# SwiGLU on one core: tile 2 of w1 held back by a dummy sigmoid, tile 3 moved behind the first w1 piece, w3's halves on both queues

## The chip, the core and the metric

One core of a Trainium2 chip runs the whole program. The metric is the device time of one execution in microseconds (us). Times inside a profile count from the first instruction of the program; that span is some 1.8 us shorter than the device time. All inputs start in HBM, and the output ends there.

Most executions of a kernel lie close together, but some are more than 1.5% above the fastest of the same kernel; these are called slow.

## The reference

```python
# x: 32x32x512, w1 and w3: 512x1792, w2: 1792x512, all bf16
gate = jnp.einsum("bsd,df->bsf", x, w1)
up   = jnp.einsum("bsd,df->bsf", x, w3)
h    = silu(gate) * up
out  = jnp.einsum("bsf,fd->bsd", h, w2)
```

The contraction over 512 is cut into four tiles of 128. "Tile 2" below means the third of these (rows 256 to 383 of w1).

## The kernel before

SP and ScalarE each own a DMA queue. The kernel loads the first 256 rows of x on both queues, then the first 512 columns of w1 and of w3 in pieces, and starts on those with half a block of x. The rest of the weights follows while TensorE is already busy.

```python
    one = nc.const_aps.tensor(1.0, [P, 1], bf16)
    table = consts.tile([P, 1], fp32, name="table")

    load_x(nc.sync, 0, 1)
    load_x(nc.scalar, 1, 2)
    load_w(nc.sync, w1_sb, w1_v, 0, FK, 0, 2)      # "w1a": tiles 0, 1, 256 KB
    nc.scalar.activation(table[:], one, SIGMOID)   # dummy: brings the sigmoid table in early
    load_w(nc.scalar, w1_sb, w1_v, 0, FK, 2, DT)   # "w1b": tiles 2, 3, 256 KB
    load_w(nc.sync, w3_sb, w3_v, 0, FK, 0, 2)      # "w3a"
    load_w(nc.sync, w3_sb, w3_v, 0, FK, 2, DT)     # "w3b"
    nc.sync.dma_start_transpose(out=xT[:, :, HB:NB], in_=x_flat[HB:NB, :])
    # ... rest of w1 and w3, the other x rows, w2, all on SP

    keep_warm(6, NB)                               # six matmuls on constants
    # ... x's first 256 rows turned on TensorE, copied to xT by VectorE and ScalarE
    for dt in range(DT):                           # 16 gate matmuls of 256 columns
        for fo in range(FK):
            project(gates[fo], w1_sb, fo, 0, HB, [dt])
    for dt in range(DT):                           # 16 up matmuls
        for fo in range(FK):
            project(ups[fo], w3_sb, fo, 0, HB, [dt])
    # ... second half of the block (needs the DMA-transposed x), then all other blocks, then w2
```

## Time and profile before

| | before |
|---|---|
| device time, median of 6 | 82.59 us (82.09 to 82.73) |
| span of the profiled execution | 80.6 us |
| TensorE busy | 75.9 us, 94% |
| w1a issued, landed | 1.20, 5.02 |
| first gate matmul | 5.07 |
| first up matmul | 6.83 |
| first 256 rows of x ready in xT | 4.1 to 4.76 |

"Issued" is the start of the issuing instruction; "landed" is that start plus the time to landing that the DMA view gives for it. TensorE never waits noticeably after 5.07, so the span is the start of the weight matmuls plus a fixed 75.5 us. The prediction below shows the lines of the chain; in it the up matmuls start at 6.99, because a piece of the chain begins where the one before it ends. TensorE's own timeline (start, length, what, in brackets the idle time before) has the start itself:

```profile
5.07 1.92 PE L123 MATMUL gate_ps<-xT,w_sb 128*128 128x256 bf16 x16 [0.94 <-DMA w_sb<-in_w_dram]
6.83 1.91 PE L123 MATMUL up_ps<-xT,w_sb 128*128 128x256 bf16 x16
```

### The profile page before, as it was taken

To read this page: it belongs to the slowest core of one execution; us is meant where nothing else is said; L and a number is where in the kernel's file an instruction comes from. 1 tells how busy PE (TensorE), PEld (TensorE's weight loads), DVE (VectorE), ACT (ScalarE), POOL (GpSimd) and SP (SyncE) were. 2 spreads that over 40 slices of the span, in tenths; PEclk is the share of its full clock that TensorE was granted. 3 is DMA by queue.
4 is the path that set the end of the run, shared out by engine and by line. 5 is a ranking of instruction groups with operands and counts; after the bars stand their busy time and mean duration, and the time that the engine had idled before them with its cause. 6 is when DMAs were issued, how large, how long until landed. Compare 5 with 4: busy or idle time off the path is not lost.

```text
span 80.6 us, 1063 instructions
## 1 busy us (share of the span) xinstructions
PE 75.9 (94%) x404; PEld 38.8 (48%) x410; DVE 39.4 (49%) x61; ACT 23.2 (29%) x39; POOL 0.7 (1%) x6
## 2 busy tenths in 40 slices
PE   6959999999999999999999999999999999999960
PEld 2348984444444444444444444444444444444850
DVE  0110189999888878878868878872000000000040
ACT  4430274223432223432223432220220220220200
POOL 3000000000000000000000000000000000000000
PEclk9999999999999999999999999999999999999999
DMA  1999999989910000000000000000101102001120
GB/s 24 271 365 273 350 370 370 295 185 355 355 47 0 0 0 0 0 0 0 8 4 0 0 0 0 0 4 0 38 27 65 41 24 73 34 31 65 36 78 17
DMA packets 9893, 7.67 MB, mean 95 GB/s; under 512 B 3744, under 2 KB 9888, under 8 KB 9888
## 3 DMA queue, kind: packets, MB, share of 16 engines
q1 hardware_dynamic: 9472, 7.21, 29.6%
q10 hardware_dynamic: 416, 0.39, 1.4%
q8 instruction: 3, 0.05, 0.3%
q14 instruction: 2, 0.02, 0.1%
HBM read 5.77 MB, written 1.05 MB: 85 GB/s over the span
## 4 chain that ended last, share of the span: by engine, by line
PE 90%; DMA 5%; issue 1%; SPq 0%; DVE 0%; DVEq 0%
PE gate_ps L123 30%; PE o_ps L171 30%; PE up_ps L123 30%; DMA w_sb<-in_w_dram 5%; SPq L62 0%; DVE o_sb L180 0%; DVEq L180 0%
## 5 line engine op out<-in xcount | busy, mean ns | idle before, releaser
L123 PEld LDWEIGHTS <-w_sb 128*128 128x128 bf16 x256 | 25.0, 98 | 24.2 <-DMA w_sb<-in_w_dram 1.1
L123 PE MATMUL gate_ps<-xT,w_sb 128*128 128x512 bf16 (+1 forms) x126 | 28.7, 352 | 1.0 <-DMA w_sb<-in_w_dram 0.9
L123 PE MATMUL up_ps<-xT,w_sb 128*128 128x512 bf16 (+1 forms) x126 | 28.7, 352 | 0.1
L133 ACT ACTIVATE sig<-gate_ps 128x512 f32<-128x512 f32 x28 | 16.7, 597 | 32.0 <-PE gate_ps L123 29.7
L171 PE MATMUL o_ps<-w_sb,hT 128*128 128x512 bf16 (+2 forms) x138 | 24.3, 336 | 0.1
L135 DVE TENSOR_TENSOR t<-gate_ps,sig 128x512 f32<-128x512 f32 x28 | 19.3, 689 | 9.5 <-ACT sig L133 9.5
L136 DVE TENSOR_TENSOR hT<-t,up_ps 128x512 bf16<-128x512 f32 x28 | 19.3, 688 | 3.3 <-PE gate_ps L123 0.5
L171 PEld LDWEIGHTS <-hT 128*128 128x128 bf16 x140 | 12.6, 98 | 12.0
L180 DVE CAST o_sb<-o_ps 128x128 bf16<-128x128 f32 (+1 forms) x3 | 1.0, 336 | 22.3 <-PE o_ps L171 22.3
L182 ACT CAST o_sb<-o_ps 128x512 bf16<-128x512 f32 x7 | 4.1, 586 | 17.9 <-PE o_ps L171 17.9
L94 PE MATMUL warm_ps<-const-bfloat16-1.0 128*128 128x512 bf16 x6 | 2.7, 626 | 0.8 <-PEq L202 0.8
L116 DVE CAST xT<-pT 128x128 bf16<-128x128 f32 (+1 forms) x2 | 0.7, 358 | 3.7 <-PE pT L106 3.7
L94 PEld LDWEIGHTS <-const-bfloat16-1.0 128*128 128x128 bf16 x6 | 0.7, 136 | 1.8 <-issue 1.8
L74 ACT ACT_TABLE_LOAD x1 | 1.3, 1283 | 1.2 <-PEq L202 1.2
L116 ACT CAST xT<-pT 128x128 bf16<-128x128 f32 (+1 forms) x2 | 0.9, 426 | 1.2 <-PE pT L106 1.2
L106 PEld LDWEIGHTS <-x_sb 128*128 128x128 bf16 x8 | 0.5, 101 | 0.9 <-DMA x_sb<-in_x_dram 0.8
L106 PE MATMUL pT<-ident,x_sb 128*128 128x128 bf16 x8 | 0.7, 230 | 0.0
masks.py:199 POOL TENSOR_SCALAR_AFFINE_SELECT ident<-ident 128x128 bf16<-128x128 bf16 x1 | 0.3, 294 | 0.1
masks.py:197 POOL MEMSET ident<- 128x128 bf16 x1 | 0.2, 205 | 0.3 <-POOLq L202 0.3
L74 ACT ACTIVATE table<-const-bfloat16-1.0 128x1 f32<-128x1 bf16 x1 | 0.2, 203 | 0.0
L202 POOL MEMSET const-bfloat16-1.0<- 128x1 bf16 x1 | 0.1, 103 | 0.0
L202 POOL MEMSET const-uint8-127<- 128x1 uint8 x1 | 0.1, 103 | 0.0
(2 smaller groups left out, 0.2 us busy)
## 6 DMA issues: line engine op xcount, KB each, us to landing
w_sb<-in_w_dram SPq DMA_DIRECT2D x2, 896.0 KB, 7.0
w_sb<-in_w_dram SPq DMA_DIRECT2D x2, 768.0 KB, 8.1
w_sb<-in_w_dram SPq DMA_DIRECT2D x2, 512.0 KB, 5.8
out_dram<-o_sb SPq DMA_DIRECT2D x7, 128.0 KB, 1.7
w_sb<-in_w_dram SPq DMA_DIRECT2D x3, 256.0 KB, 4.3
w_sb<-in_w_dram ACTq DMA_DIRECT2D x1, 256.0 KB, 4.0
x_sb<-in_x_dram ACTq DMA_DIRECT2D x1, 128.0 KB, 2.8
x_sb<-in_x_dram SPq DMA_DIRECT2D x1, 128.0 KB, 2.6
```

Of the source, the lines that this page charges most:

```text
L74: nc.scalar.activation(table[:], one, SIGMOID)
L94: nc.tensor.matmul(warm_ps[:, 0:cols], lhsT=one.to_broadcast([P, P]), rhs=one.to_broadcast([P, cols]), start=True, stop=True,)
L106: nc.tensor.matmul(pT[:, i, j, :], lhsT=x_sb[:, nt, dt * P : (dt + 1) * P], rhs=ident[:], start=True, stop=True,)
L116: copy(xT[:, dts[0] : dts[-1] + 1, nts[0] * P : (nts[-1] + 1) * P], pT[:].rearrange("p d t c -> p d (t c)"),)
L123: nc.tensor.matmul(ps[:, c0 : c0 + n1 - n0], lhsT=w_sb[:, dt, fo * P : (fo + 1) * P], rhs=xT[:, dt, n0:n1], start=(dt == 0), stop=(dt == D ...
L133: nc.scalar.activation(sig[:], gate_ps[:], SIGMOID)
L135: nc.vector.tensor_mul(t[:], gate_ps[:], sig[:])
L136: nc.vector.tensor_mul(hT[:, fo, nb * NB : (nb + 1) * NB], t[:], up_ps[:])
L171: nc.tensor.matmul(o_ps[:], lhsT=hT[:, fo, nt * P : (nt + 1) * P], rhs=w2_sb[:, fo, c0 : c0 + DB], start=(fo == 0), stop=(fo == FT - 1),)
L180: nc.vector.tensor_copy(o_sb[:], o_ps[:])
L182: nc.scalar.copy(o_sb[:], o_ps[:])
L202: nc = _bacc.Bacc("TRN2", target_bir_lowering=False, num_devices=1)
```

## The change

The intent: w1a is what TensorE waits for, and it shares the DMA engines with a piece that is needed later. So the later piece is held back. Tile 2's load is made to wait for the dummy sigmoid, by letting that sigmoid write into tile 2's place; tile 3 goes behind w1a on SP; and w3's first half goes behind tile 2 on ScalarE's queue.

```diff
-    table = consts.tile([P, 1], fp32, name="table")
-
+
+    nc.scalar.activation(w1_sb[:, 2, 0:1], one, SIGMOID)
     load_x(nc.sync, 0, 1)
     load_x(nc.scalar, 1, 2)
     load_w(nc.sync, w1_sb, w1_v, 0, FK, 0, 2)
-    nc.scalar.activation(table[:], one, SIGMOID)
-    load_w(nc.scalar, w1_sb, w1_v, 0, FK, 2, DT)
-    load_w(nc.sync, w3_sb, w3_v, 0, FK, 0, 2)
+    load_w(nc.scalar, w1_sb, w1_v, 0, FK, 2, 3)
+    load_w(nc.sync, w1_sb, w1_v, 0, FK, 3, DT)
+    load_w(nc.scalar, w3_sb, w3_v, 0, FK, 0, 2)
     load_w(nc.sync, w3_sb, w3_v, 0, FK, 2, DT)
```

## The prediction

> **What bounds the kernel now.** I read the chain that ended last first, because it says which engine the end hangs on. All times are us from the span's start.
>
> ```profile
> PE 90%; DMA 5%; issue 1%; SPq 0%; DVE 0%; DVEq 0%
> ...
> 1.20 3.83 DMA w_sb<-in_w_dram
> 5.02 0.05 issue
> 5.07 1.92 PE gate_ps L123 x16
> 6.99 1.75 PE up_ps L123 x16
> ```
>
> The first line is the page's summary, the others the start of the chain in order of time (start, length, what). From 5.07 to 78.0 the chain is matmul after matmul; TensorE's longest later wait does not show at all. So the time is "when the first weight matmul starts" plus about 73 us of back-to-back matmuls plus a 2.6 us tail. The change reorders only loads in the first microseconds, so it can move only that start, or open a new gap behind it. The start is set by one DMA: the first w1 piece (contraction tiles 0 and 1, 256 KB, called w1a), issued on the SP queue at 1.20 and landed at 5.02.
>
> Next the timeline of the first five microseconds, to see what else could set the start (start, length, engine; a trailing q is a queue's issue).
>
> ```profile
> 0.73 0.40 ACTq L62 DMA_DIRECT2D x_sb<-in_x_dram  x1
> 1.17 1.28 ACT L74 ACT_TABLE_LOAD   x1 [1.17 <-PEq L202]
> 1.23 0.44 ACTq L66 DMA_DIRECT2D w_sb<-in_w_dram  x1
> 2.46 0.20 ACT L74 ACTIVATE table<-const-bfloat16-1.0 128x1 f32<-128x1 bf16 x1
> 3.84 0.92 ACT L116 CAST xT<-pT 128x128 bf16<-128x128 f32 x2 [1.17 <-PE pT L106]
> ...
> 3.72 0.66 DVE L116 CAST xT<-pT 128x128 bf16<-128x128 f32 x2 [3.72 <-PE pT L106]
> ```
>
> The transposed x is there early: both parts of contraction tile 0 by about 4.1 (ScalarE's first, short copy), tile 1 at 3.72+0.66 = 4.38, tiles 2 and 3 at 3.84+0.92 = 4.76. Thus w1a at 5.02 is the last arrival, 0.9 us behind its partner. That 0.9 us, 1.1% of 82.7, is the most the change can win: even a w1a that landed at once would leave the start at about 4.15.
>
> Third, the DMA view in windows, to see why w1a takes 3.83 us. Columns are the window, each engine's busy time, clock, DMA share, GB/s; then, for 3.0 to 4.5 alone, packets, MB and share per queue (q1 is SP's, q10 ScalarE's).
>
> ```profile
> 1.50:2.00 0.50, 0.50 (x2) 0.15 (x1) 0.00 (x0) 0.50 (x1) 0.00 (x0) 1.00 0.52 92
> 2.00:2.50 0.50, 0.50 (x3) 0.22 (x2) 0.00 (x0) 0.49 (x2) 0.00 (x0) 1.00 0.67 129
> 2.50:3.00 0.50, 0.50 (x3) 0.09 (x1) 0.00 (x0) 0.16 (x1) 0.00 (x0) 1.00 1.10 322
> 3.00:3.50 0.50, 0.50 (x3) 0.10 (x1) 0.00 (x0) 0.00 (x0) 0.00 (x0) 1.00 0.89 268
> 3.50:4.00 0.50, 0.50 (x8) 0.40 (x7) 0.28 (x2) 0.16 (x1) 0.00 (x0) 1.00 1.06 367
> 4.00:4.50 0.50, 0.14 (x3) 0.00 (x0) 0.38 (x2) 0.43 (x2) 0.00 (x0) 1.00 1.07 373
> ...
> q1 hardware_dynamic: 268, 0.26, 53.0%
> q10 hardware_dynamic: 254, 0.24, 47.7%
> ```
>
> Half a microsecond times 92+129+322 GB/s is 271 KB: by 3.0 the two x tiles (2 x 131 kB) have just gone through. From 3.0 to 4.5 the engines are full and split evenly: 0.26 MB for SP, which is all of w1a (262 kB), and 0.24 MB for ScalarE's queue, which is its w1 piece (tiles 2 and 3). The second is needed only eight matmuls later, yet takes half of the rate while w1a is in flight. This is what the change attacks.
>
> **What the Trainium skill says.** "DMA: Bandwidth & Descriptors", section "Issuing engines are not separate DMA queues", says that DMAs from either engine share the same 16 DMA engines and interleave; the even split of 0.26 to 0.24 MB agrees. "ScalarE: Activation LUTs", section "What ACT_TABLE_LOAD costs", gives about 1283 ns for the load; the trace has 1.28 us. It adds a drain of about 1380 ns, which this trace does not show, as the dummy sigmoid starts at 2.46, right at the load's end. "Perfetto Trace Analysis", section on the HWDGE DMA instruction, says that a DMA's semaphore wait is done on its sequencer before the profiled issue starts. No instruction in this region waits so before the change, so no view here shows it; the new wait depends on it. The same section says the descriptor generator is locked for one user at a time. The trace shows no such cost for plain loads: SP's and ScalarE's x issues, started at 0.74 and 0.73, take 0.39 and 0.40 side by side.
>
> **The change part by part.**
>
> (1) Table load and dummy sigmoid go to the head of ScalarE, before its x load. In the before trace the w1 load was issued at 1.23 while the table load ran from 1.17, so an engine instruction does not hold up the issue of a DMA behind it. Two more entries cost about 1.23-1.13 = 0.1 us. So the table load should start near 0.75 and end near 2.03, the sigmoid end near 2.24, and ScalarE's x load be issued near 0.82 instead of 0.73. It lands at 3.5 before; up to 0.1 later moves transposes and copies by at most 0.1 (tiles 2 and 3 ready at 4.85), still ahead of w1a.
>
> (2) The sigmoid writes into column 0 of tile 2's place, so that tile's load (128 KB, w1c) must wait for it: a delay made from a true dependency. It is issued near 2.28 instead of 1.23. First bytes come 1.0 us after an issue (SP's x issue at 0.74, first bytes of the span at 1.75), and a little later on ScalarE: so near 3.4.
>
> (3) w1a thus has the engines to itself from 3.0 to 3.4, instead of sharing them throughout. At 268 to 350 GB/s (the measured ramp and the plateau) that moves 107 to 140 kB of its 262. The rest, 122 to 155 kB, goes at half of 370 GB/s: 0.66 to 0.84 us, so last bytes at 4.06 to 4.24. Landing comes some 0.5 to 0.6 us after last bytes (before: last bytes near 4.4, landed 5.02). **w1a lands at 4.55 to 4.85, midpoint 4.7, against 5.02: 0.3 us won.** A cleaner hold of w1c would win up to 0.6.
>
> (4) Tile 3 (128 KB) goes to SP behind w1a, and w3's first half moves to ScalarE's queue behind w1c. The sum of bytes up to the end of w3 is the same. What matters is each due time. With a start at 4.75 and 0.11 us per 256-column matmul (16 gate matmuls from 5.07 to about 6.83 before): tile 2 is due at 4.75+8x0.11 = 5.6 and lands near 4.7 to 4.9; tile 3 due at 6.1, lands near 5.4; w3's first half due at 6.5. w3's first half now shares with w1 tile 3 and with w3's second half. From about 4.15, 262 kB at half rate take 1.4 us: last bytes 5.6, landed 6.2. That is 0.3 before it is due; before, it landed at 1.66+4.3 = 5.96 and was due at 6.83, so 0.9 of slack falls to 0.3. w3's second half (due 7.4, lands near 6.7) and the DMA-transposed x (before: issued 2.67, landed 5.1 later at 7.8, due at 8.57; now due at 8.25) keep some slack. The weights after these land 2.7 us and more ahead.
>
> Sum: start 5.07 to about 4.75, nothing behind it stalls, so **-0.3 us**, with ScalarE, VectorE and the later loads on no path. The executions on record are 82.72, 82.73 and 82.09, so -0.3 is inside the run-to-run spread. From the centre of these (82.5 to 82.7) I get 82.3.
>
> **The rivals.**
>
> Nothing gained (82.6): the loads are bound by total bytes, and w3's first half becomes the wait that ends last. For it: both halves of w3 now finish together, and before the second one landed only at 2.16+4.6 = 6.76. If the first half takes until then, TensorE waits at 6.5 and the gain shrinks to about 0.05. Against it: the second half queues behind tile 3 on SP.
>
> More gained (81.9): the single SP ring runs at full rate at once and w1c's data comes after 3.7, so w1a lands near 4.3 and the start falls to the floor of 4.15 to 4.4 that the x copies set. For it: from 5.0 to 5.75 SP alone moved 352 GB/s, so one queue fills the engines. Then slack of the DMA-transposed x (0.77 us) would cap the gain near 0.7.
>
> Lost (83.0): ScalarE's issues block. Its w3 issue near 2.7 falls on SP's transposing issue (2.67, 1.30 long). If the generator lock holds it until 3.97, ScalarE's two copies, which stand behind it in program order, start near 4.4, and tiles 2 and 3 of x come at 5.35. The start would still be near 4.75, so even this costs at most a few tenths. A table load that held the x issue until 2.2 would be worse: x at 5.0, start near 5.9, +0.8 us. The issue at 1.23 during the load speaks against that.
>
> **Range and chances.** No rival moves the time by 2% (1.65 us): the floor allows -0.9, and the worst loss I can construct is +0.8. The range is the gain of 0 to 0.7 with the spread of executions around it: 81.8 to 82.8. Within 2% gets 0.96, and the rest is split in favour of faster.
>
> **What would show it.** In the changed profile: table load first on ScalarE near 0.75; w1c's issue near 2.3; w1a 3.3 to 3.6 us from issue to landing instead of 3.83; first gate matmul at 4.5 to 4.9; no idle stretch on TensorE between the gate and up matmuls. I am wrong if ScalarE's x copies end after 5, if TensorE waits for w_sb before the up matmuls or for xT before the second gate halves, or if w1a still lands at 5.0.

## The result, and the profile after

The changed kernel takes 83.79 us in the median (83.61 to 85.3). The ratio of its fast runs to those of before is 1.0158, with a 95% interval of 1.0119 to 1.0197: 1.3 us slower. A ratio is the mean time of one kernel's fast runs over that of the other's of the same rounds (here 83.79 over 82.48), so it is not quite the ratio of the medians. The measured time lies outside the predicted range.

The first trace of the changed kernel fell into a slow execution (span 83.5 us, mean granted clock 0.98). I use it for the landings of the loads, all issued by 2.64 us and long before its clock column falls at 6.9, and take the account of time from a second trace of the same kernel, made among the experiments (84.09 us, span 82.3, clock 1.00, state unknown).

First, the chain that ended last in the second trace of the changed kernel (start, length, what):

```profile
2.26 0.34 ACTq L66
2.61 0.03 issue
2.64 5.79 DMA w_sb<-in_w_dram
8.42 0.05 issue
8.47 1.92 PE up_ps L123 x16
```

Before, the DMA of the chain was w1a, issued at 1.20. Now it is a load issued by ScalarE at 2.64, w3's first half, which lands at 8.42. The up matmuls start at 8.47, against 6.83 before: 1.64 us later. The span grew from 80.6 to 82.3, which is 1.7. So nothing after the first up matmul matters.

Second, TensorE's own timeline of the same execution (start, length, what, and in brackets the idle time before; the window ends at 9.0, hence the x5):

```profile
4.23 1.92 PE L123 MATMUL gate_ps<-xT,w_sb 128*128 128x256 bf16 x8
6.85 1.05 PE L123 MATMUL gate_ps<-xT,w_sb 128*128 128x256 bf16 x8 [0.70 <-DMA w_sb<-in_w_dram]
8.47 0.72 PE L123 MATMUL up_ps<-xT,w_sb 128*128 128x256 bf16 x5 [0.58 <-DMA w_sb<-in_w_dram]
```

The first gate matmul runs at 4.23, 0.84 us earlier than before: the intended gain is there, and more of it than I had hoped. Then TensorE has used up w1a and waits for tile 2 until 6.85, and again for w3 until 8.47. (The first eight took 1.92 us, about twice what they need; the stall behind them hides that. More on it under the experiments.)

The loads tell the same. Landings in us from the span's start:

| load | before | predicted | after, first trace | after, second trace |
|---|---|---|---|---|
| w1a (tiles 0, 1) | 5.02 | 4.55 to 4.85 | 4.32 | 4.17 |
| w1 tile 2 | 5.27 (w1b) | 4.7 to 4.9 | 7.24 | 6.80 |
| w1 tile 3 | 5.27 (w1b) | 5.4 | 5.66 | 6.54 |
| w3a | 5.95 | 6.2 | 8.22 | 8.42 |
| w3b | 6.78 | 6.7 | 7.38 | 7.90 |
| DMA-transposed x | 7.80 | by 8.25 | 8.98 | 9.17 |

w1a was rushed by 0.7 to 0.85 us. Everything behind it is 0.4 to 2.5 us late. It isn't a matter of order alone, since even the last of them is 1.2 to 1.4 us late, although the bytes are the same. The DMA engines must have moved less. The windows view shows where; its columns are the window, its length, each engine's busy time and instructions (PE, PEld, DVE, ACT, POOL), and the last three are TensorE's granted clock, the mean busy share of the DMA engines, and GB/s. Before:

```profile
1.50:4.00 2.50, 2.50 (x13) 0.96 (x11) 0.28 (x2) 1.31 (x3) 0.00 (x0) 1.00 0.85 236
4.00:5.50 1.50, 0.56 (x7) 0.40 (x5) 0.38 (x2) 0.69 (x2) 0.00 (x0) 1.00 1.07 369
```

The changed kernel, first trace:

```profile
1.50:4.00 2.50, 2.47 (x13) 0.92 (x11) 0.29 (x1) 0.82 (x3) 0.00 (x0) 1.00 0.74 239
4.00:5.50 1.50, 1.25 (x12) 0.72 (x9) 0.42 (x1) 0.75 (x2) 0.00 (x0) 1.00 0.77 176
```

And its second trace:

```profile
1.50:4.00 2.50, 2.50 (x11) 1.05 (x10) 0.29 (x1) 0.89 (x3) 0.00 (x0) 1.00 0.88 245
4.00:5.50 1.50, 1.50 (x11) 1.10 (x9) 0.42 (x1) 0.69 (x2) 0.00 (x0) 1.00 0.84 214
```

Up to 4.0 the sum is the same in all: 2.5 us times 236 to 245 GB/s, or 0.59 to 0.61 MB. Rushing w1a moved no more bytes; it only moved other bytes. From 4.0 to 5.5, where the kernel before runs at 369 GB/s, the changed one gets 176 and 214. That is 1.5 us times some 155 to 193 GB/s, 0.23 to 0.29 MB short, which at 369 GB/s takes 0.6 to 0.8 us to make up. The busy share falls too (0.77 and 0.84 for 1.07), although loads issued at 1.65 and 2.15 are pending. It falls by less than the rate because some packets take longer: by an estimate from share and packets (588 before, 282 in the first trace of the changed kernel), a packet took 44 ns in the mean before and 66 after, while the median is 46 in both. This trough is the thing to be explained. It is not the whole delay: from 5.5 to 7.0 the second trace moves 235 GB/s, against 280 before.

### The profile page after: what moved, and what is told of

Same layout as the page of the kernel before. It is cut to its first block, busy times and chain, and to the rows that moved or that the text cites. A ratio compares the mean times of both kernels' runs of the same rounds, so it can differ in the third digit from the quotient of the medians.

```text
span 83.5 us, 1064 instructions
## 1 busy us (share of the span) xinstructions
PE 77.6 (93%) x404; PEld 39.5 (47%) x410; DVE 39.4 (47%) x61; ACT 23.2 (28%) x39; POOL 0.7 (1%) x6
## 3 DMA queue, kind: packets, MB, share of 16 engines
HBM read 5.77 MB, written 1.05 MB: 82 GB/s over the span
## 4 chain that ended last, share of the span: by engine, by line
PE 88%; DMA 6%; issue 2%; ACT 1%; DVE 0%; DVEq 0%
PE up_ps L123 30%; PE gate_ps L123 29%; PE o_ps L171 29%; DMA w_sb<-in_w_dram 6%; ACT L70 1%; DVE o_sb L180 0%; ACT w_sb L70 0%; DVEq L180 0%
## 5 line engine op out<-in xcount | busy, mean ns | idle before, releaser
L123 PEld LDWEIGHTS <-w_sb 128*128 128x128 bf16 x256 | 25.6, 101 | 26.3 <-DMA w_sb<-in_w_dram 2.5
L123 PE MATMUL gate_ps<-xT,w_sb 128*128 128x512 bf16 (+1 forms) x126 | 29.7, 361 | 2.1 <-DMA w_sb<-in_w_dram 2.0
L123 PE MATMUL up_ps<-xT,w_sb 128*128 128x512 bf16 (+1 forms) x126 | 29.4, 359 | 0.1
```

The costliest lines, as they stand in the source:

```text
L123: nc.tensor.matmul(ps[:, c0 : c0 + n1 - n0], lhsT=w_sb[:, dt, fo * P : (fo + 1) * P], rhs=xT[:, dt, n0:n1], start=(dt == 0), stop=(dt == D ...
```

## The experiments

Twenty traces in all were compared: two of before, two of the changed kernel, and sixteen of others. Five of the others are single executions; the profiled executions without the wait (first trace), with the transpose later, of the wait alone, of the split only and of the single tiles were slow ones. Their loads are read, not their times. The trough doesn't rest on them: w3a back on SP, all on SP, late w3a and few big loads show it in fast executions. The theories carry letters in the expectations, and came up in this order. A: a load that ScalarE issues near 2.3 us is held back by the DMA transpose that SP issues at 2.6. B: w3a on ScalarE's queue crowds tile 2 out. C: any load after an idle stretch of a queue is slow to start. D: the table load ahead of the x loads slows the loads. E: chance, the loads differ from one execution to the next. F: the split of w1b and both queues for w3. G: a load issued late on ScalarE slows both queues. H: SP alone can't be fed fast enough. I: late issue as such. J: rushing one piece makes the loads behind it lag. K and L refine J.

### The wait taken out

Changed kernel, but the sigmoid writes to a tile of its own:

```diff
-    nc.scalar.activation(w1_sb[:, 2, 0:1], one, SIGMOID)
+    table = consts.tile([P, 1], bf16, name="table")
+    nc.scalar.activation(table[:], one, SIGMOID)
```

> The changed kernel, but the dummy sigmoid writes to a tile of its own, so no load waits. Theory A (a load issued on ScalarE's queue near 2.3 us is held back by the transposing DMA that SP issues at 2.6 us): tile 2's load is issued near 1.25, lands by 5.0, no stall of TensorE above 0.2 us, time 0.3 to 0.6 us below the kernel before. Rival B (w3's first half on ScalarE's queue crowds tile 2 out): the stall of about 2 us stays, +1 us. Rival C (any load after an idle stretch of the queue is slow to start): as A here, since the queue is not idle.

Measured: 84.2 us in the median, ratio 1.0163 (1.0056 to 1.027), its four times spread from 83.19 to 85.2. Tile 2 landed at 4.95, as A said, but w1a now at 5.68 and the transposed x at 8.82. So a loss stays without the wait, in another place. A is not the whole reason. A second trace of the same kernel:

> The changed loads without the wait, dummy sigmoid at the head, a second trace. Its first trace showed w1's first piece at 5.68 and the transposed x at 8.82 without any late issue, which theory G does not explain. If that trace was an unlucky execution, this one shows the transposed x by 7.9 and w1's first piece by 5.2; if it is the kernel, again near 8.8.

It was no accident: w1a landed at 5.01 this time, but w3a at 7.95 and the transposed x at 9.15, with 246 GB/s between 4.0 and 5.5 (312 in the first trace). But this kernel's time isn't the loads' doing alone. In both traces all 16 gate matmuls took twice their time (3.59 and 3.60 us for 1.92; more under the split only):

```profile
5.05 3.60 PE L124 MATMUL gate_ps<-xT,w_sb 128*128 128x256 bf16 x16 [0.58 <-DMA w_sb<-in_w_dram]
```

By an estimate from the landings, with gate matmuls at full speed the up matmuls would have started at 7.5 in the first trace (w1a's 5.73 plus 1.76) and at 8.0 in the second (w3a's landing), against 6.83 before: 0.7 and 1.2 us are left for the loads.

### The DMA transpose moved away

Changed kernel, with the transpose behind the next load:

```diff
+    load_w(nc.sync, w1_sb, w1_v, FK, 8)
     nc.sync.dma_start_transpose(out=xT[:, :, HB:NB], in_=x_flat[HB:NB, :])
-    for c0, c1 in ((FK, 8), (8, FT)):
-        load_w(nc.sync, w1_sb, w1_v, c0, c1)
-        load_w(nc.sync, w3_sb, w3_v, c0, c1)
+    # ... the three other loads, in the old order
```

> The changed kernel, but the first transposing DMA is issued behind the next 512 KB w1 load on SP. Theory A: tile 2's load, still issued near 2.27, lands 2.5 to 2.9 us later (near 5.0), and the 2 us stall ahead of it is gone; a new stall of 0.5 to 1.5 us may come ahead of the second half of x, whose load is now behind 512 KB more. Rival C: tile 2 still lands near 7.2 and the 2 us stall stays, with the stall for x on top or hidden in it.

Measured: tile 2 landed at 7.34, as before the move; three of four executions were slow, the fast one took 85.29 us, so there is no interval. SP's transpose at 2.6 is not what holds tile 2 back. A falls. (Another load of SP stands in its place; the transpose itself is issued at 3.19.)

### w3's first half back on SP

```diff
-    load_w(nc.scalar, w3_sb, w3_v, 0, FK, 0, 2)
+    load_w(nc.sync, w3_sb, w3_v, 0, FK, 0, 2)
```

> The changed kernel, but w3's first half goes back to SP, so tile 2 is alone on ScalarE's queue after x and waits as before. Theory A: the transposing DMA is now issued some 0.5 us later (near 3.1), so tile 2's load is half out of its way: it lands between 5 and 6.5, stall 0 to 1.2 us. Rival B: it lands by 5.0 and the stall is gone, time 0.3 us or more below before. Rival C: lands near 7.2, stall of 2 us, +1 us.

Measured: ratio 1.0101 (1.0034 to 1.0167); tile 2 landed at 6.66. Some 0.5 us of the loss may be w3a's place on ScalarE's queue, going by the difference to 1.0158, but the intervals overlap, so this isn't shown. The stall ahead of tile 2 remains, so B explains a part at most.

### The wait alone

Kernel before, with the sigmoid at the head and writing into tile 2's place, so that the whole 256 KB of w1b waits:

```diff
-    table = consts.tile([P, 1], fp32, name="table")
+    nc.scalar.activation(w1_sb[:, 2, 0:1], one, SIGMOID)
 ...
-    nc.scalar.activation(table[:], one, SIGMOID)
```

> The kernel before, with only the dummy sigmoid moved to the head and writing into tile 2's place, so ScalarE's 256 KB load waits for it. Theory A: this load, issued near 2.27 next to the transposing DMA, lands past 6.5, and TensorE stalls between its eighth and ninth gate matmul for 1 to 2 us; time +0.5 to +1.5 us. Rival B: no stall above 0.3 us. Rival C: as A.

Measured: w1b, issued at 2.26, landed at 7.70; three of four executions were slow, the fast one took 83.77 us. The wait by itself (the moved table load alone costs nothing, see below) is enough for a loss, as far as one fast run can show it. And w1a landed at 5.13 here, though its only company was SP's own next load.

### Second traces, and the move of the table load alone

> The kernel before again, for a second trace. Theory E (the loads' engines lag differently from one execution to the next): the first w1 piece lands anywhere between 4.5 and 5.6, the transposed x between 7.6 and 8.9. Theory D (moving the table load ahead of the x loads slows the loads): as in the first trace, w1 near 5.0 and the transposed x near 7.8, within 0.2.

w1a landed at 4.89, the transposed x at 7.71. [The first trace had 5.02 and 7.80.] Chance as large as E has it isn't seen in the kernel before.

> The changed kernel again, for a trace in the fast state. Theories A and D: tile 2 lands past 6.5 again and the transposed x near 9.0, stall of 1.3 us or more ahead of the ninth gate matmul; without the halved TensorE clock the gate matmuls after the stall come 0.11 us apart and the time is near 83.7. Theory E: tile 2's landing moves by 0.5 us or more from the first trace's 7.24.

Tile 2 landed at 6.80 instead of 7.24, the transposed x at 9.17 instead of 8.98. TensorE's idle time was 0.70 us, or 1.6 from where full-speed matmuls would have ended (4.23 plus 1.05): it is the kernel, and the account above is from this trace.

The table load moved alone (kernel before, sigmoid in its own tile at the head):

```diff
+    nc.scalar.activation(table[:], one, SIGMOID)
     load_x(nc.sync, 0, 1)
 ...
-    nc.scalar.activation(table[:], one, SIGMOID)
```

> The kernel before, with the dummy sigmoid (own tile) moved ahead of ScalarE's x load and nothing else. Theory D: as slow as the runs with that move: the transposed x lands near 8.7 instead of 7.8 and the time rises by 0.4 us or more. Theory A and a fifth, F (splitting w1's second piece and using both queues for w3 is what hurts): no change, within 0.2 us of before.

Measured: ratio 0.9982 (0.9925 to 1.0038), w1a at 4.71, the transposed x at 7.77. D falls. As this was the only version that looked at all better than before, it ran once more:

> The kernel before with only the dummy sigmoid moved to the head, in more rounds: the one version of these that may beat both. Its trace had w1's first piece 0.3 us earlier. If that is the kernel's doing: 0.1 to 0.4 us below before, interval below 1. If it was chance: within 0.1 us of before.

Ratio 0.9981 (0.9924 to 1.0037). w1a landed at 4.71 again, so the loads are steadily 0.2 to 0.3 us earlier than before. But the time isn't shown to be better, and TensorE's timelines of the two traces show why the gain doesn't come through each time. First trace, then second:

```profile
4.75 1.92 PE L123 MATMUL gate_ps<-xT,w_sb 128*128 128x256 bf16 x16 [0.23 <-DMA w_sb<-in_w_dram]
```

```profile
4.75 2.83 PE L123 MATMUL gate_ps<-xT,w_sb 128*128 128x256 bf16 x16 [0.21 <-DMA w_sb<-in_w_dram]
```

The same 16 matmuls, started at the same moment, took 1.92 us in an execution of 82.08 us and 2.83 in one of 82.99. In the second, the matmuls that began before 6.66 ran at half speed. Its six times lie in two clusters, 81.93 to 82.00 and 82.66 to 82.99.

### The new loads without the move and without the wait

Tile 2 on ScalarE, tile 3 on SP, w3 on both queues, but the sigmoid in its old place behind ScalarE's x load:

```diff
-    nc.scalar.activation(w1_sb[:, 2, 0:1], one, SIGMOID)
+    table = consts.tile([P, 1], bf16, name="table")
     load_x(nc.sync, 0, 1)
     load_x(nc.scalar, 1, 2)
+    nc.scalar.activation(table[:], one, SIGMOID)
```

> The changed kernel's loads (tile 2 on ScalarE, tile 3 on SP, w3 on both queues) but with the dummy sigmoid in its own tile and in its old place behind ScalarE's x load, so no wait and no move. Theory D: the gain first hoped for, 0.1 to 0.5 us below before. Theory F: like the run without the wait, 0.7 us or more above before.

Measured: ratio 1.0002 (0.9928 to 1.0076) over its two fast runs; two others were slow (84.34 and 84.83). F falls. w1a landed at 5.19, so it was not rushed, and the DMA engines did not starve:

```profile
4.00:5.50 1.50, 0.82 (x8) 0.49 (x6) 0.49 (x2) 0.80 (x2) 0.00 (x0) 1.00 1.06 365
```

What the two slow executions are is seen in the trace, which is of the first of them:

```profile
5.24 3.60 PE L124 MATMUL gate_ps<-xT,w_sb 128*128 128x256 bf16 x16 [0.68 <-DMA w_sb<-in_w_dram]
```

All 16 gate matmuls ran at half speed, 3.60 us for 1.92, which is 1.7 us and nearly all of its distance to the fast runs. The clock column reads 1.00 in that stretch all the same, but it says nothing there: the trace's first clock record begins at 8.86, and the view counts time without a record as full clock. The matmuls agree with the records. They come 213 ns apart up to 8.84 and 109 ns from 8.96 on; in the second trace of the moved table load the step and the first record are both at 6.66, and in those without the wait at 9.97 and 9.26 (first record 10.05 and 9.26).

This run and the one without the wait differ only in whether the table load stands ahead of ScalarE's x load or behind it. Alone that move costs nothing, together with the new loads the rate between 4.0 and 5.5 was lower in two traces of two (312 and 246 for 365). I can't explain this.

### All weights on SP

```diff
-    load_w(nc.scalar, w1_sb, w1_v, 0, FK, 2, DT)
+    load_w(nc.sync, w1_sb, w1_v, 0, FK, 2, DT)
```

(Against the kernel before.)

> All weights on SP in the order of their use, ScalarE's queue with its x tile alone, no wait. Theory G (a load that ScalarE issues while SP's later loads are being set up, at 2.3 us instead of 1.2, slows both queues for some 2 us): nothing is issued late on ScalarE, so SP runs at 340 GB/s or more from 3.0 on: w1's first piece lands near 4.2, its second near 5.0, the transposed x by 7.9; time 0.4 to 0.8 us below before. Theory H (SP alone cannot be fed faster than about 250 GB/s from 3.5 us on, whatever ScalarE does): w1's first piece near 4.2, the second past 5.3, the transposed x near 8.7, a stall, and the time between 0.2 below and 0.8 above before.

Measured: ratio 1.0054 (1.0015 to 1.0093). w1a landed at 4.21, w1b at 6.71, the transposed x at 9.16, and:

```profile
4.00:5.50 1.50, 1.47 (x15) 0.97 (x13) 0.68 (x2) 0.85 (x2) 0.00 (x0) 1.00 0.85 234
```

There is no wait, nothing late on ScalarE, nothing on its queue but x, and the trough is there. G falls as the needed cause, and H's numbers nearly hold. (SP's later loads are issued 0.5 us later than before; a run below does the same without a trough.) The same, with w3a on ScalarE's queue and made to wait for the sigmoid:

```diff
-    nc.scalar.activation(table[:], one, SIGMOID)
+    nc.scalar.activation(w3_sb[:, 0, 0:1], one, SIGMOID)   # at the head
-    load_w(nc.sync, w3_sb, w3_v, 0, FK, 0, 2)
+    load_w(nc.scalar, w3_sb, w3_v, 0, FK, 0, 2)
```

> As the run with all weights on SP, but w3's first half is issued by ScalarE and waits for the dummy sigmoid at the head, so it goes out near 2.27. w1 is wholly on SP. Theory G: that late issue slows SP's own loads: w1's second piece, w3's second half or the transposed x land 0.5 us or more later than with all on SP, w3's first half lands past 6.8, TensorE stalls ahead of the up matmuls, time 0.3 us or more above before. Theory H: SP's loads land as with all on SP or earlier, since SP has 256 KB less to issue.

Ratio 1.0140 (1.0089 to 1.0191). w1b landed at 6.91 (6.71 with all on SP), the transposed x at 8.87 (9.16): SP's loads land about as with all on SP, though SP had 256 KB less to move, and the late one landed at 7.91. And with w3a issued early instead, by writing the sigmoid to a tile of its own:

> As the run with the late w3 half, but without the wait, so ScalarE issues it near 1.25. Theory G: no slow stretch between 3.5 and 5.5 us (340 GB/s or more), the transposed x by 7.9, but w1's first piece lands near 5.0 as it shares again. Theory H: the transposed x near 8.7.

82.53 us in a single execution, w1a at 5.09, the transposed x at 7.73, 362 GB/s between 4.0 and 5.5. With 256 KB on the other queue from 1.22 on, w1a isn't rushed, and nothing starves. H falls in its plain form, since SP carries the same first three loads here.

### Each tile by itself, all issued early

Kernel before, with w1's tiles alternating between the queues and w3 as one load:

```diff
-    load_w(nc.sync, w1_sb, w1_v, 0, FK, 0, 2)
+    load_w(nc.sync, w1_sb, w1_v, 0, FK, 0, 1)
     nc.scalar.activation(table[:], one, SIGMOID)
-    load_w(nc.scalar, w1_sb, w1_v, 0, FK, 2, DT)
-    load_w(nc.sync, w3_sb, w3_v, 0, FK, 0, 2)
-    load_w(nc.sync, w3_sb, w3_v, 0, FK, 2, DT)
+    load_w(nc.scalar, w1_sb, w1_v, 0, FK, 1, 2)
+    load_w(nc.sync, w1_sb, w1_v, 0, FK, 2, 3)
+    load_w(nc.scalar, w1_sb, w1_v, 0, FK, 3, DT)
+    load_w(nc.sync, w3_sb, w3_v, 0, FK)
```

> w1's four tiles one by one, alternating between SP (0 and 2) and ScalarE (1 and 3), w3 as one 512 KB load on SP, no wait; everything up to w3 is issued by 2.6. Theory I (what counts is when a load is issued: its bytes come 2 us or more after that, so issuing late on any queue leaves the DMA engines short): no window between 3.5 and 6 below 300 GB/s, tile 0 lands near 4.4, the transposed x by 7.9, time 0.2 to 0.7 us below before. Theory J (whenever one piece is rushed to land before 4.5, the loads behind it lag for other reasons): a window below 240 GB/s between 3.5 and 5.5, the transposed x past 8.5, time at or above before.

Ratio 1.0132 (1.0077 to 1.0187). Tiles 0 and 1 landed at 4.06 and 4.26, but tile 3 at 6.60 and w3 at 9.11:

```profile
4.00:5.50 1.50, 1.50 (x11) 1.18 (x9) 0.42 (x1) 0.72 (x2) 0.00 (x0) 1.00 0.95 268
```

The weights up to w3 were issued by 2.12, earlier than in the changed kernel, and it didn't help. (The profiled execution is a slow one, 84.77 us.) Nor is the window shown the whole of it: from 7.0 to 8.5 the engines moved only 37 GB/s in this trace, with w3 still to land. A version with few and large loads behind the first two tiles (tiles 2 and 3 together on SP, w3 whole on ScalarE):

> Six loads, all issued by 2.2: w1 tile 0 on SP, tile 1 on ScalarE, then tiles 2 and 3 together on SP beside the whole of w3 (512 KB) on ScalarE. Theory I: no window between 3.5 and 6 below 300 GB/s, tiles 0 and 1 near 4.4, tiles 2 and 3 near 5.6 with a stall of at most 0.5 us, time 0 to 0.6 us below before. Theory J: a window below 240 GB/s and time above before.

Two of four executions were slow; the fast ones took 83.08 and 84.03 us. Tiles 0 and 1 landed at 4.06 and 4.30, tiles 2 and 3 at 6.56, 285 GB/s between 4.0 and 5.5. I falls in both, and J comes closer: the loads behind lag in both, and the few big loads fall to 186 GB/s between 4.0 and 4.5, though the single tiles stay at 250 or more in every half microsecond, above J's 240.

### Late on SP, and late on ScalarE with SP quiet

Kernel before, with the head sigmoid writing into w3's place, so that SP's w3a waits:

```diff
-    table = consts.tile([P, 1], fp32, name="table")
+    nc.scalar.activation(w3_sb[:, 0, 0:1], one, SIGMOID)
 ...
-    nc.scalar.activation(table[:], one, SIGMOID)
```

> The kernel before, but the dummy sigmoid is at the head and writes into w3's place, so that SP's first w3 load is issued near 2.27 instead of 1.66 and all behind it 0.5 us later; w1 is untouched, nothing is late on ScalarE. Theory I: w1's pieces land as before (5.0 and 5.3), but the rest some 0.5 us later (w3 near 6.5 and 7.3, the transposed x near 8.3), with a window below 300 GB/s between 4.5 and 6. If the time of issue did not matter while earlier loads are in flight: as before, transposed x near 7.8, no such window.

w3a went out at 2.25, and the engines kept going:

```profile
4.00:5.50 1.50, 1.19 (x8) 0.73 (x7) 0.42 (x1) 0.66 (x2) 0.00 (x0) 1.00 1.05 346
```

w1a landed at 4.67, w3a at 6.37, the transposed x at 8.12, each in time for its matmuls. A load issued at 2.25 behind others isn't late in itself, at least in this one execution. (The single time, 82.95, includes gate matmuls that took 2.83 us, half-speed ones again.)

The last of these asks why tile 2, issued at 2.27, was so slow to begin. SP is kept quiet until 4.4 by a memset on VectorE behind the x copies, into tile 3's place. w3a leaves ScalarE's queue too and follows on SP:

```diff
+    nc.vector.memset(w1_sb[:, 3, 0:1], 0.0)         # after the x copies
     load_w(nc.sync, w1_sb, w1_v, 0, FK, 3, DT)      # and all of SP's later loads behind it
```

> Slow on purpose: as the changed kernel, but SP issues nothing between w1's first piece and 4.5 us (its next load waits for a VectorE memset behind the x copies), and w3 goes out on SP after that. So tile 2's load, issued by ScalarE near 2.27, meets no other issue and, after 3.7, no other data. If its late first bytes (near 4.3 in all runs with the wait) came from sharing with SP's issues: first bytes near 3.4, landed by 4.2. If any load issued then takes 2 us to start: first bytes near 4.3, landed near 4.9.

The DMA view from 3.3 to 4.3 us shows packets, MB and engine share of each queue that moved anything (q10 is ScalarE's). Changed kernel, second trace:

```profile
q1 hardware_dynamic: 284, 0.27, 110.1%
```

With SP quiet:

```profile
q10 hardware_dynamic: 139, 0.13, 41.2%
q1 hardware_dynamic: 124, 0.11, 31.9%
```

In the changed kernel ScalarE's queue moved nothing at all in that microsecond, so tile 2's first byte came more than 2.0 us after its issue at 2.26. With SP quiet, all 0.13 MB of tile 2 went through by 4.3. The issue groups of the DMA view, of each issue alone, give its time to landing in us, first in the changed kernel (second trace), then with w3a back on SP (the run above, where tile 2 also has ScalarE's queue to itself behind x), then with SP quiet:

```profile
w_sb<-in_w_dram ACTq DMA_DIRECT2D x1, 128.0 KB, 4.5
```

```profile
w_sb<-in_w_dram ACTq DMA_DIRECT2D x1, 128.0 KB, 4.4
```

```profile
w_sb<-in_w_dram ACTq DMA_DIRECT2D x1, 128.0 KB, 2.5
```

This part is shown, by a single execution: the same load, with the same wait, issued at the same time, takes 2.5 us where SP has nothing set up behind w1a, and 4.4 to 5.1 in the four other traces where SP has three or more transfers pending. The waiting isn't in the sigmoid, nor in an idle queue (C falls), nor in w3a behind it, but in the company of SP's pending loads. Which part of the hardware they share isn't shown. (The kernel is slow on purpose: 84.22 us.)

### One long load

```diff
-    load_w(nc.sync, w1_sb, w1_v, 0, FK, 0, 2)
+    load_w(nc.sync, w1_sb, w1_v, 0, FK)
     nc.scalar.activation(table[:], one, SIGMOID)
-    load_w(nc.scalar, w1_sb, w1_v, 0, FK, 2, DT)
-    load_w(nc.sync, w3_sb, w3_v, 0, FK, 0, 2)
-    load_w(nc.sync, w3_sb, w3_v, 0, FK, 2, DT)
+    load_w(nc.sync, w3_sb, w3_v, 0, FK)
```

> SP alone with x, then the whole first w1 block as one 512 KB load, then the w3 block as one; ScalarE's queue has x alone. Both are issued by 2.2. In the run with w1 in two pieces on SP the rate fell to 170 to 210 GB/s between 3.5 and 5.0, as the second piece began. Theory K (a load that has to begin before about 4.2 behind two others on its queue is not ready): one long load has no such beginning, so 340 GB/s or more from 3.0 to 4.5, w1 whole near 5.1, and the transposed x near 7.9; time within 0.3 us of before. Theory L (one queue alone cannot hold more than about 384 KB in flight that early): the rate falls at 3.7 here too, w1 lands past 5.8, time 0.7 us or more above before.

```profile
3.50:4.50 1.00, 0.62 (x8) 0.45 (x8) 0.54 (x2) 0.42 (x2) 0.00 (x0) 1.00 1.08 371
4.50:5.50 1.00, 0.20 (x2) 0.19 (x3) 0.08 (x1) 0.43 (x1) 0.00 (x0) 1.00 0.87 282
```

SP alone holds 371 GB/s through the stretch where it fell to about 170 to 200 with w1 in two pieces, so L falls: it isn't the bytes in flight. The rate falls when the next load begins, now at 4.5. But K put the limit at 4.2, and the transposed x came at 8.68, not 7.9, so K holds only in part. The single time was 83.39, some 1 us above before and not within K's 0.3.

### What the traces say together

| | first w1 piece landed | GB/s from 4.0 to 5.5 |
|---|---|---|
| before (2 traces), table load moved (2), split only, early w3a, late w3a on SP | 4.67 to 5.19 | 340 to 369 |
| changed (2), transpose later, w3a back on SP, all on SP, late w3a on ScalarE, tiles, few big loads | 4.06 to 4.32 | 176 to 285 |
| wait taken out (2), wait alone, one long load | 5.01 to 5.68 | 246 to 312 |

From 1.5 to 4.0 these 19 traces differ little: 227 to 256 GB/s, or 0.57 to 0.64 MB. (The twentieth, with SP quiet, is left out.) In eight of eight where the first piece landed before 4.4, the rate was then 285 GB/s or less. The reverse does not hold: in the last row it was low without that, two times clearly (246 and 253) and two times less (308 and 312). So rushing is a sufficient sign, in these kernels, and not the mechanism. No version beat the kernel before by more than the noise.

## Why the prediction was wrong

**What bounds the kernel, and w1a's sharing: right.** w1a did share its rate, and alone it landed at 4.17 to 4.32. ("Split evenly" is true only of the sum from 3.0 to 4.5: SP's queue moved 0.16 MB to ScalarE's 0.06 up to 3.75, and 0.10 to 0.18 after that, so it was w1a's last part that was slowed.) The gain of part (3) was mis-sized in the good direction, 0.7 to 0.85 us for 0.3, because tile 2 did not join it at 3.4.

**Part (1): right.** The table load started at 0.74, ScalarE's x load was issued at 0.80, tiles 2 and 3 of x were ready at 4.82 in the first trace. In the second they were ready at 5.06, past the prediction's sign of 5; TensorE's turning of x took 1.16 us for 0.75 before; nothing waited for them. The move alone costs nothing (ratio 0.998). The fear that a table load holds up an x issue did not come true.

**Part (2): the issue right, the first bytes wrong.** Tile 2 was issued at 2.27, right behind the sigmoid's end at 2.24. "First bytes come 1.0 us after an issue" was read from the very first loads, when nothing else was pending. With SP quiet it held (bytes well before 4.3, landed after 2.5 us); in the changed kernel nothing came for over 2.0 us.

**Part (4) is the step that failed:** the rate at which the loads behind w1a come in. "The sum of bytes up to the end of w3 is the same" is true, and from it I took half of 370 GB/s for each of two queues. The sum of the rates was 176 and 214 GB/s from 4.0 to 5.5. With that, w3a came at 8.42 where I had 6.2, and was due at 6.5; the slack of 0.3 us was no match. It is the prediction's own sign of being wrong, "if TensorE waits for w_sb before the up matmuls", that came. I had read the 352 GB/s of SP alone between 5.0 and 5.75 as a property of a queue. It isn't one: with all weights on SP the rate fell to 168 between 4.0 and 4.5. What lets a queue hold its rate when its next load begins isn't shown. It isn't simply how long that load had been pending: late w3a on SP, issued at 2.25, was followed by 346 GB/s, and w1's second piece, issued by SP at 1.68, by 234.

**The rivals.** "Nothing gained" named the right load, w3's first half, as the wait that ends last, but had it land by 6.76 instead of 8.42. "More gained" had w1a right and the rest wrong. "Lost" had the sign right for a wrong reason: ScalarE's w3 issue took 0.49 us (2.64 to 3.13) beside SP's transposing issue (2.63 to 4.00), and its copies were not delayed. The "worst loss I can construct", 0.8 us, was too small because every construction kept the DMA engines full. That no rival moves the time by 2% did come true (1.0158).

**What stays open.** Shown are the trough, that in the changed kernel TensorE waits for the loads that it delays, that neither the wait, the transpose at 2.6, the table load at the head, w3a on ScalarE's queue nor a late issue on ScalarE is needed for it, and, by one execution, that tile 2's own lag is due to SP's pending transfers. Not shown is what the pending transfers wait for (the transpose is among them by 3.21 us in all nineteen traces of the table, so its part in the trough was not tested), why the table load's place matters only together with the split, and whether a rushed first piece causes the trough or is another sign of the same thing.

## What to carry to other kernels

A rate that one queue reached in a settled stretch is not a rate at which its next load begins; when a change makes a load due earlier, a rate taken from later in the old trace doesn't say when it will land. Holding back one transfer to speed another is worth it only if the engines stay full behind it, so compare the sum over both queues, window by window, and not the landing of the piece that was rushed. Where the start of a kernel is already within a few tenths of its partner's arrival, the other loads' slack is the budget, and it is soon spent.

## What the Trainium skill lacked or had wrong

- "DMA: Bandwidth & Descriptors", section "Latency and other measured facts": it gives about 600 ns to the first byte for loads from SP and ScalarE. Here the first x bytes came 1.0 us after the start of their issue (0.74 to 1.75), which is 0.6 after its end (1.13), so the figure agrees if it is counted from there. Tile 2's came more than 2.0 us after the start, or 1.7 after the end (2.60), with SP's loads pending. The page's row has no such case.
- The same page, section "Issuing engines are not separate DMA queues": it says that issuing from several engines saves only the issue time. The split of the data agrees (0.26 to 0.24 MB), but with all weights on SP the engines moved 234 GB/s between 4.0 and 5.5, against 369 with the two queues of the kernel before. That spreading can also decide whether the engines starve early in a kernel isn't in that section.
- "Perfetto Trace Analysis", section on the HWDGE DMA instruction: that the semaphore wait ends before the profiled issue begins agrees (sigmoid's end 2.24, issue 2.27). The exclusive lock on the descriptor generator was not visible in the issue times: 0.49 us for ScalarE's w3 issue beside SP's transposing issue of 1.37.
- "TensorE: Matmul & The Clock Gate", Part 1 ("The HAM clock gate"): it says that the clock halves after an idle window of about 3.4 us, free-running, and that the warm-up varies from run to run. The variation agrees: the same 16 matmuls took 1.92, 2.83 or 3.60 us, and the 3.60 is most of the slow split-only execution. The halving came sooner than the page lets one expect: in the first trace of the changed kernel TensorE went idle at 5.4, and the clock column fell at about 6.9, after 1.5 us of idleness; the 3.4 us before that fall held 1.05 us of gate matmuls. The line below is its window from 7.0; the column before the last two is the clock.

```profile
7.00:7.50 0.50, 0.21 (x2) 0.15 (x3) 0.00 (x0) 0.00 (x0) 0.00 (x0) 0.50 0.86 156
```

- No page says that the clock column of this profile view can read 1.00 while matmuls run at half speed, because the trace has no clock record there (split only: first record at 8.86, matmuls 213 ns apart before it and 109 after).
